# A Fourier mixing and gated feed-forward kernel: the third of the first-level products is split again

## Chip, cores and metric

The kernel runs on one core of one Trainium2 chip. The metric is device time in microseconds (us).

## What is computed

```python
X = np.fft.fft(x, axis=1)              # x: (8, 3008, 256) float32
X = np.fft.fft(X, axis=2)
x2 = X.real.reshape(24064, 256)
h = x2 @ w_in                          # w_in: (256, 2048)
g = h * (1.0 / (1.0 + np.exp(-1.702 * h)))
out = g @ w_out                        # w_out: (2048, 256)
```

## The kernel before

The second Fourier transform is folded into `w_in` once, at the start (`wcs`). The first one is done for batch b+1 while the feed-forward of batch b runs, in small matmul groups: first-transform groups (`mix1`, four per batch) and second-transform groups (`stage2`, three per batch, one for each block of output frequencies). `rotate` (the column turn) fixes one column of the first transform's result with a small matmul and a copy by ScalarE before the next batch's first `stage2`.

The main loop runs over 384 steps t = (batch b, block blk, half hh, p). Eight steps, p = 0 to 7, make a group: one output tile of 256 frequency columns (226 in the groups with blk 0 and hh 1, called narrow below) and their mirror columns. A step computes two blocks of 128 hidden features for both sides, and what it adds to the output is done LAG = 3 steps later. Steps 0 to 7 and the last eight work in simpler ways; steps 8 to 375 are called deep: 46 groups, 184 pairs of steps.

In a step t each engine has its own queue, in program order:

- TensorE (PE): `begin(t, 1)` and `begin(t + 1, 0)`, the two halves of the hidden matmuls into the PSUM banks x (tags b0 and b1, by turns); `product(t - 3)`; the small products of a pair; a transform group, if the step has one.
- ScalarE (ACT): `forward` (L649), `doubled` (L646), `activate_back` (L656), then `middle(t + 2)` (L634, twice), which writes the bank x of step t + 2 with a starting value. It can do so only when `backward(t)` has read that bank.
- VectorE (DVE): `backward(t)` (L653) subtracts to give the mirror side; `sums` (L671, L672) makes the sums S2 and S4 of a pair of steps; `deeper` makes the second-level sums, in two parts (L695 and L697, then L699 one step later).
- GpSimd: `sums` (L664, L665) makes S1 and S3; the folds of the first transform.

The output matmul uses products by the seven-for-eight scheme (Strassen's in Winograd's form), on 2 by 2 blocks. At the first level there are seven products per step: of A11, S2, S3 with weights each 128 by 128, and of the four operands A12, S4, A22, S1. For those four the pair of steps is split again in the same way: `small_products` does seven products (numbered 1 to 7) of 64 by 128 blocks for each of them, from the raw halves of operands and from the sums in `big[SUM:]`. They add up in the PSUM tile `low` (three banks) and part of bank o1 during a group. The first three are done by `product`, on all 256 columns.

At a group's end `combine` copies and adds the first-level results (L810, L813, L814); in the next step, the one whose product opens the next group, `combine_small` reads the second-level results from `low` (L842, four operations). `swap` (L850 to L852, ScalarE) exchanges partition halves; `combine_last` (L824, L860), `turn_last` and `store` finish two to four steps later.

Transform groups need PSUM banks for a short time. They take the banks of `low`, and bank b2, in the second step of a group, when `low` has just been read. Nearly every group has one there. Such a step is called special; in it the small products of the running pair are put off, and the step after it (`after`) does all seven at once. 36 of the 46 group ends are followed by a special step (21 hold a `stage2`, 13 two `mix1`, one a `mix1`, one a `stage2` and a `mix1`), 10 are not. The order is written out by hand; nothing reorders it.

## Time and profile before

| | |
|---|---|
| median of 3 runs | 1838.43 us (1836.69 to 1840.38) |
| the profiled execution | 1838.17 us, its span 1836.0 us |
| granted TensorE clock, mean | 1.0 |
| VectorE, busy | 1476.7 us, 80% |
| ScalarE, busy | 1137.6 us, 62% |
| GpSimd, busy | 991.0 us, 54% |
| L653 (`backward`), waiting for ScalarE's L649 | 143.0 us, 174 times |
| L695 (`deeper`), waiting for small products | 86.6 us, 115 times |
| L842 (`combine_small`), waiting for small products | 31.6 us, 45 times |

Busy times are those of one execution. A matmul is shown with the span from its start to its modelled end, and they overlap; what a group of them takes is read from the start of one group to the start of the next. A float32 matmul shows as two instructions in the counts. DVE and ScalarE operations also overlap their neighbour a little, so the same holds there. Idle time of an engine that isn't the bottleneck costs nothing.

### The profile page before, as it was taken

Reading aid. Unit: us, or ns where it says so; the run is one execution under the profiler, and the core shown is the slowest. Engines: PE = TensorE matmul, PEld = TensorE weight load, DVE = VectorE, ACT = ScalarE, POOL = GpSimd, SP = SyncE. Lnnn points to the kernel's source line nnn. Section 1 sums busy time; section 2 is a strip of 40 time slices with the busy share of each in tenths; the row PEclk is TensorE's granted clock in tenths of the full one; section 3 lists DMA queues with packets and bytes.
Section 4 is the critical chain, followed back from the end, with each engine's and each line's share of the span. In section 5 each row is a group of like instructions: output and inputs, shape, how many; then the busy total and the mean of one; then the engine's idle time right before and its main releaser. Section 6 shows DMA issues by size and latency. Waiting matters only on the chain.

```text
span 1836.0 us, 55861 instructions
## 1 busy us (share of the span) xinstructions
PE 1820.3 (99%) x23656; PEld 1403.6 (76%) x23656; DVE 1476.7 (80%) x1927; ACT 1137.6 (62%) x2238; POOL 991.0 (54%) x1070
## 2 busy tenths in 40 slices
PE   8999999999999999999999999999999999999998
PEld 5677778777777777777778777787777877777775
DVE  7988878887888778887887878878788787878874
ACT  4566656666666656666666666666665666656663
POOL 3785556553656546565456644666446653444442
PEclk9999999999999999999999999999999999999999
DMA  8811160214211151212402024020331102100011
GB/s 272 195 52 35 44 115 20 64 26 100 56 48 36 42 117 23 61 35 67 88 13 75 24 67 86 15 80 18 86 67 30 31 18 65 29 20 13 18 24 24
DMA packets 151687, 105.68 MB, mean 58 GB/s; under 512 B 106212, under 2 KB 133094, under 8 KB 150878
## 3 DMA queue, kind: packets, MB, share of 16 engines
q1 hardware_dynamic: 148270, 99.09, 22.3%
q8 instruction: 186, 3.05, 0.7%
q10 hardware_dynamic: 3168, 3.03, 0.6%
q14 instruction: 63, 0.52, 0.1%
HBM read 64.81 MB, written 48.05 MB: 61 GB/s over the span
## 4 chain that ended last, share of the span: by engine, by line
PE 96%; DMA 2%; DVE 1%; ACT 0%; issue 0%; POOL 0%; DVEq 0%; ACTq 0%; POOLq 0%
PE x L196 35%; PE o L196 27%; PE low L740 25%; PE o L740 4%; PE low L273 1%; PE low L393 1%; DMA big<-in_moe_w_in_dram 1%; DMA xt<-in_x_dram 1%; PE po L196 0%; PE pa L196 0%; PE pb L196 0%; POOL xt L905 0%; DVE big L751 0%; PE low L196 0%; PE psw L533 0%
## 5 line engine op out<-in xcount | busy, mean ns | idle before, releaser
L664 POOL TENSOR_TENSOR big<-big 128x256 f32<-128x256 f32 (+1 forms) x376 | 364.7, 970 | 787.6 <-ACT big L656 776.9
L196 PE MATMUL x<-pq,wcs 128*64 128x256 f32 (+1 forms) x6016 | 769.7, 375 | 0.4 <-ACT x L634 0.4
L196 PE MATMUL o<-big,wo 128*64 128x256 f32 (+1 forms) x4800 | 635.3, 376 | 0.3 <-DVE big L671 0.3
L196 PEld LDWEIGHTS x<-pq,wcs 128*64 128x64 f32 x6016 | 427.0, 137 | 172.6 <-issue 1.2
L196 PEld LDWEIGHTS o<-big,wo 128*64 128x64 f32 x4800 | 340.3, 137 | 146.6 <-issue 10.0
L646 ACT ACTIVATE g<-x 128x512 f32<-128x512 f32 (+1 forms) x376 | 221.7, 590 | 363.5 <-PE x L196 362.4
L665 POOL TENSOR_TENSOR big<-big 128x256 f32<-128x256 f32 (+1 forms) x376 | 381.1, 1014 | 0.0
L740 PE MATMUL low<-big 128*64 128x128 f32 (+1 forms) x5888 | 379.8, 270 | 0.0
L649 ACT ACTIVATE big<-x 128x512 f32<-128x512 f32 (+1 forms) x376 | 221.8, 590 | 237.4 <-PE x L196 211.3
L653 DVE TENSOR_TENSOR big<-g,x 128x512 f32<-128x512 f32 (+1 forms) x376 | 250.8, 667 | 143.4 <-ACT big L649 143.0
L634 ACT ACTIVATE x<-nb,af 128x256 f32<-128x256 f32 (+1 forms) x752 | 352.7, 469 | 12.2
L740 PEld LDWEIGHTS low<-big 128*64 128x64 f32 x5888 | 337.2, 137 | 24.7
L695 DVE TENSOR_TENSOR big<-big 128x1024 f32<-128x1024 f32 (+1 forms) x184 | 225.2, 1224 | 108.4 <-PE low L740 86.6
L656 ACT ACTIVATE big<-big 128x512 f32<-128x512 f32 (+1 forms) x376 | 231.5, 616 | 27.4 <-DVE big L653 26.1
L740 PE MATMUL low<-big,wo 128*64 128x128 f32 (+1 forms) x2944 | 222.4, 270 | 0.1
L699 DVE TENSOR_TENSOR big<-big 128x512 f32<-128x512 f32 (+1 forms) x184 | 191.6, 1041 | 0.0
L740 PEld LDWEIGHTS low<-big,wo 128*64 128x64 f32 x2944 | 174.4, 137 | 6.6 <-DVE big L699 0.6
L697 DVE TENSOR_TENSOR big<-big 128x512 f32<-128x512 f32 (+1 forms) x184 | 166.6, 906 | 16.0
L672 DVE TENSOR_TENSOR big<-big 128x512 f32<-128x512 f32 (+1 forms) x188 | 158.9, 845 | 6.5
L842 DVE TENSOR_TENSOR big<-big,low 128x512 f32<-128x512 f32 (+3 forms) x184 | 109.1, 610 | 35.1 <-PE low L740 31.6
L671 DVE TENSOR_TENSOR big<-big 128x512 f32<-128x512 f32 (+1 forms) x188 | 131.6, 700 | 0.9 <-POOL big L664 0.9
L740 PE MATMUL o<-big,wo 128*64 128x128 f32 (+1 forms) x1472 | 111.2, 270 | 0.0
(119 smaller groups left out, 1105.1 us busy)
## 6 DMA issues: line engine op xcount, KB each, us to landing
out_dram<-os SPq DMA_DIRECT2D x284, 64.0 KB
Td<-xt SPq DMA_DIRECT2D x56, 192.0 KB
t<-Td SPq DMA_DIRECT2D x21, 512.0 KB
xt<-in_x_dram SPq DMA_DIRECT2D x14, 512.0 KB
xt<-Xr SPq DMA_DIRECT2D x14, 512.0 KB
nb<-Nd SPq DMA_DIRECT2D x22, 256.0 KB
out_dram<-os SPq DMA_DIRECT2D x96, 56.0 KB
Xr<-in_x_dram SPq DMA_DIRECT2D x7, 752.0 KB
```

The source lines that it names most:

```text
L196: nc.tensor.matmul(out[c0:c0 + 64], lhsT=lhs[:, c0:c0 + 64], rhs=rhs, skip_group_check=True, **how)
L634: nc.scalar.activation(x[:, i * 256:i * 256 + n], nbt[b, blk][:, hh * 256:hh * 256 + n], ACTF.Copy, scale=af1[:, f:f + 1])
L646: nc.scalar.activation(two(g[:], n), two(xb[t][:], n), ACTF.Copy, scale=2.0)
L649: nc.scalar.activation(front(t), two(xb[t][:], width(t)), ACTF.Gelu_apprx_sigmoid)
L653: nc.vector.tensor_tensor(back(t), two(gt.pop(t)[:], n), two(xb.pop(t)[:], n), op=ALU.subtract)
L656: nc.scalar.activation(back(t), back(t), ACTF.Gelu_apprx_sigmoid)
L664: eng.tensor_tensor(right(t, S1, n), left(t, A21, n), right(t, A22, n), op=ALU.add)
L665: eng.tensor_tensor(left(t, S3, n), left(t, A11, n), left(t, A21, n), op=ALU.subtract)
L695: nc.vector.tensor_tensor(free(big[:], SUM, *both_), free(big[:], from11 + w, *twice), free(big[:], from11, [at_right(t, 0) + w - from11, ...
L697: nc.vector.tensor_tensor(s2, a11, s1, op=ALU.subtract)
L699: nc.vector.tensor_tensor(s4, a12, s2, op=ALU.subtract)
L740: nc.tensor.matmul(o, lhsT=lhs, rhs=rhs, start=first_in, stop=(p == NP - 2), skip_group_check=True)
```

## The change

The product of S3 also goes to the second level. S3 moves from the left operands to the right ones (five operands for four in `raws`, `made_sum` and `deeper`), with its own seven small products, `lone_products`. They fill one PSUM bank, `lone`, which is the bank b2; product 7 is split into two column halves, so that each side of the array gets the same work. `lone_weights` makes the weight sums once. At a group's end `move_lone` (seven ScalarE copies) and `combine_lone` (five VectorE operations) put the result together into the output sum, and `combine_last` gets one more addition. `combine` loses one (L814) in deep groups. Transform groups now take `low` and `lone`; `rotate` stands ahead of `stage2` in the special step itself. The output tile has one buffer for two, and the back operand two slots for four. The core of the diff:

```diff
-    op = ctx.enter_context(tc.tile_pool(name="op", bufs=2, space=SB))
+    op = ctx.enter_context(tc.tile_pool(name="op", bufs=1, space=SB))
...
-    LEFT, MADE, RIGHT, SUM, RES, OUT = 0, 4096, 8192, 14336, 16384, 18432
-    A11, A21, S3, S2 = range(4)
-    A12, S4, A22, S1 = range(4)
+    LEFT, BACK, OUT, SPARE, MADE, RIGHT, SUM, RES = 0, 2048, 2560, 3584, 4096, 8192, 15872, 18432
+    A11, S2 = range(2)
+    A12, S4, A22, S1, S3 = range(5)
...
+    def at_back(t):
+        return BACK + t % 2 * 256
...
-            eng.tensor_tensor(right(t, S1, n), left(t, A21, n), right(t, A22, n), op=ALU.add)
-            eng.tensor_tensor(left(t, S3, n), left(t, A11, n), left(t, A21, n), op=ALU.subtract)
+            a21 = big[:, at_back(t):at_back(t) + n]
+            eng.tensor_tensor(right(t, S1, n), a21, right(t, A22, n), op=ALU.add)
+            eng.tensor_tensor(right(t, S3, n), left(t, A11, n), a21, op=ALU.subtract)
...
-            both_, twice = ([512, 2], [128, 4], [1, w]), ([0, 2], [256, 4], [1, w])
+            both_, twice = ([640, 2], [128, 5], [1, w]), ([0, 2], [256, 5], [1, w])
             nc.vector.tensor_tensor(free(big[:], SUM, *both_), free(big[:], from11 + w, *twice),
-                                    free(big[:], from11, [at_right(t, 0) + w - from11, 2], [256, 4], [1, w]), op=ALU.subtract)
+                                    free(big[:], from11, [at_right(t, 0) + w - from11, 2], [256, 5], [1, w]), op=ALU.subtract)
...
+    ALONE = {2: (0, 0), 3: (0, 1), 4: (128, 0), 5: (128, 1), 1: (256, 0), 6: (256, 1), 7: (384, 0)}
+
+    def lone_products(t, ks):
...
+        for k in ks:
+            c0, side = ALONE[k]
...
+            part = (w + 1) // 2
+            for side_, lo, hi in ((0, 0, part), (1, part, w)) if k == 7 else ((side, 0, w),):
+                nc.tensor.matmul(pot["lone"][64 * side_:64 * side_ + 64, c0:c0 + hi - lo], lhsT=lhs, rhs=rhs[:, lo:hi],
+                                 start=opens(p, 5, side_), stop=(p == NP - 2), skip_group_check=True)
...
-            plan = [(0, 0, wo[:, p, 0, :], left(t, A11, n)), (0, 1, wt[:, p, 0, :], left(t, S2, n)),
-                    (1, 0, wt[:, p, 1, :], left(t, S3, n))]
+            plan = [(0, 0, wo[:, p, 0, :], left(t, A11, n)), (0, 1, wt[:, p, 0, :], left(t, S2, n))]
...
+    def move_lone(t):
...
+        nc.scalar.copy(across[64:128], ps[0:64, 256:256 + w])
+        nc.scalar.copy(across[0:64], ps[64:128, 256:256 + w])
+        nc.scalar.copy(begun[0:64], ps[0:64, 256:256 + w])
+        for to in (0, 64):
+            nc.scalar.copy(whole[to:to + 64, 0:part], ps[0:64, 384:384 + part])
+            nc.scalar.copy(whole[to:to + 64, part:], ps[64:128, 384:384 + w - part])
+
+    def combine_lone(t):
...
+        nc.vector.tensor_tensor(u, across, ps[:, 256:256 + w], op=ALU.add)
+        nc.vector.tensor_tensor(begun[64:128], u[64:128], ps[64:128, 128:128 + w], op=ALU.add)
+        nc.vector.tensor_tensor(u, u, whole, op=ALU.add)
+        nc.vector.tensor_tensor(oc[:, 2, 0:w], begun, ps[:, 0:w], op=ALU.add)
+        nc.vector.tensor_tensor(oc[:, 2, w:2 * w], u, ps[:, 128:128 + w], op=ALU.add)
...
@@ def combine_last(t):
+        nc.vector.tensor_tensor(oc[:, 2, :n], oc[:, 1, :n], oc[:, 2, :n], op=ALU.add)
         fifth(free(big[:], RES + 768, [0, 2], [1, n]), n)
...
@@ main loop
+            if t > NP:
+                spare[:] = ["l0", "l1", "l2", "l3"]
+                for fn, args in extra.get(t, ()):
+                    if fn is rotate:
+                        fn(*args)
...
             if opening:
                 small_products(t - LAG - 1, other[:2])
+                lone_products(t - LAG - 1, (1, 6))
...
             if not after:
                 small_products(t - LAG - 1, other[2 * opening:])
+                lone_products(t - LAG - 1, (2, 3) if opening else (1, 6, 2, 3))
...
             if after:
                 small_products(t - LAG - 1, (7, *other, 1, 2, 4))
+                lone_products(t - LAG - 1, (7, 1, 6, 2, 3, 4, 5))
             elif not special:
                 small_products(t - LAG, one)
+                lone_products(t - LAG, (7, 4, 5))
...
+            if t == seconds_late:
+                nyquist(1, 0, f"b{t % 2}")
             if t + 2 < n:
                 middle(t + 2)
+            move_lone(t - LAG - 1)
...
             combine_small(t - LAG - 1)
+            combine_lone(t - LAG - 1)
...
             sums(t - 1, nc.vector)
             turn_seconds()
             deeper(t - 2, 0)
             deeper(t - 3, 1)
```

## Prediction

> **What bounds the kernel now.** I read the page first, then the list of waits of each engine, then the timelines of DVE, ScalarE and TensorE around one group end. The page:
>
> ```profile
> span 1836.0 us, 55861 instructions
> ...
> PE 1820.3 (99%) x23656; PEld 1403.6 (76%) x23656; DVE 1476.7 (80%) x1927; ACT 1137.6 (62%) x2238; POOL 991.0 (54%) x1070
> ...
> PE 96%; DMA 2%; DVE 1%; ACT 0%; issue 0%; POOL 0%; DVEq 0%; ACTq 0%; POOLq 0%
> ```
>
> TensorE (PE) sets the end: busy 1820.3 of 1836.0 us, 96% of the chain. Less matmul work shortens the run only where PE still never waits, so the question is how near the other engines are to making it wait. DVE is next, at 80%; an average hides clumps. Its clump is at a group end. Call S the step whose product opens a new group, T3 the moment when PE reaches the first hidden matmuls of step S+3 (in step S+2). One such place, DVE, ScalarE and PE timelines (start, duration):
>
> ```profile
> 729.80 2.46 DVE L842 TENSOR_TENSOR big<-big,low 128x512 f32<-128x512 f32 x4 [0.80 <-PE low L740]
> 732.18 1.22 DVE L695 TENSOR_TENSOR big<-big 128x1024 f32<-128x1024 f32 x1
> 733.43 0.69 DVE L697 TENSOR_TENSOR big<-big 128x512 f32<-128x512 f32 x1
> 734.04 0.68 DVE L653 TENSOR_TENSOR big<-g,x 128x512 f32<-128x512 f32 x1
> ...
> 740.61 1.03 DVE L697 TENSOR_TENSOR big<-big 128x512 f32<-128x512 f32 x1
> 741.57 1.21 DVE L824 TENSOR_TENSOR big<-big 128x512 f32<-128x512 f32 x1
> ```
>
> ```profile
> 734.76 0.63 ACT L656 ACTIVATE big<-big 128x512 f32<-128x512 f32 x1 [0.41 <-DVE big L653]
> 735.30 0.97 ACT L634 ACTIVATE x<-nb,af 128x256 f32<-128x256 f32 x2
> ```
>
> ```profile
> 729.15 0.61 PE L740 MATMUL low<-big,wo 128*64 128x128 f32 x8
> 729.59 1.46 PE L196 MATMUL o<-big,wo 128*64 128x256 f32 x12
> 730.88 1.03 PE L196 MATMUL x<-pq,wcs 128*64 128x256 f32 x8
> 731.74 1.03 PE L196 MATMUL o<-big,wo 128*64 128x256 f32 x8
> 732.61 1.03 PE L196 MATMUL x<-pq,wcs 128*64 128x256 f32 x8
> ...
> 736.90 1.03 PE L196 MATMUL x<-pq,wcs 128*64 128x256 f32 x8
> ```
>
> DVE runs without a gap from 729.80 to the subtraction of step S+1 (L653, 734.04); that frees an x bank; ScalarE, in order, does L656 and then the two L634 that prefill the bank, ending at 736.27; PE wants it at 736.90. The chain is hidden by 0.63 us. It is the same place in every group. From the trace I took the end of the second L634 and the start of the matmuls: the cover (median) is 0.73 us where step S+1 holds a second-transform group, 1.40 where it holds two first-transform groups (1.05 in the 226-wide groups), 0.67 where it holds neither; in an ordinary step 1.2.
>
> **PE: what the change saves.** Per pair of deep steps the S3 product goes from 8 matmul instructions on 256 columns (0.865 us for eight, 731.74 to 732.61) to 12 on 128 columns (0.44 us for eight, 729.15 to 729.59) and 4 on 64. No row has 64 columns; bounds are the one-column matmuls of `first_row` (16 in 0.58 us, 26 ns each) and the 128-column ones, 55 ns. I take 28, since half of 55 is above that floor. After: 12 × 55 + 4 × 28 = 0.77; saved 0.093 us per pair (0.10 to none at the two ends). 152 pairs of 256 and 32 of 226 give 14.1 + 2.6 = 16.8 us.
>
> **DVE and ScalarE: what it adds at each pair.** The three sums of `deeper` handle five operands for four. From L697's 0.69 for 512 and L695's 1.22 for 1024, one element costs 1.04 ns: +0.27 for the first, +0.13 each for the others. In ordinary steps DVE waits 0.8 us for PE ahead of L695, or 0.3 to 2 us for ScalarE ahead of L653, which covers it. If that cover were gone, 184 × 0.53 = 98 us is the price. GpSimd does the same two operations per step; its L665 ends over 2 us before the L653 that will now wait for it, two steps on.
>
> **What it adds at a group end.** Between L842 and the sums stand five new DVE operations on 128 columns. L842 takes 0.414 for 256 and 0.687 for 512, so 0.28 each; each but one depends on the one before (start to start up to 0.1 more, as L824 to L860 shows beyond its length). I take 1.35 for the five, between 1.0 (0.2 each) and 1.6. The first waits for seven small ScalarE copies; these follow L634 (ending 1.62 us after L842 began) and take 0.26 (128 columns, from 0.365 for 256 and 0.585 for 512) and 0.2, overlapping by 0.1 as L810 and L812 do: about 0.85, so ready at 2.5; 0.17 us lost against 2.38. With 0.27 + 0.13 for the longer sums, step S+1's subtraction comes 1.93 us later after L842's start: 6.17 for 4.24. ScalarE's 2.22 us to the end of L634 follow, and 0.05 to PE.
>
> PE meanwhile gets there sooner: after the last small product that starts L842 it lacks two S3 halves of 0.43 us in S and S+1 and has two lone products (0.21) more: 0.65 earlier in steps with transform groups (their lone products are put off to S+2), 0.33 without (another 0.32 of lone products). So PE's wait at T3 is 1.93 + 0.65 + 0.05 − cover:
> - second-transform group alone, 21 group ends: 1.90 × 20, and 0.36 for the first (cover 2.27): 38.4
> - two first-transform groups, 13: 1.23 × 7, and 1.35 × 6 in narrow ones (1.75 + 0.60 + 0.05 − 1.05): 16.7
> - one first-transform group, or one of each, in the first batch: 2.09 + 1.46 = 3.6
> - neither, 10: there ScalarE, not DVE, ended 0.44 later, so the cover is 1.11: 1.20 × 8, 1.55 for a narrow one, nothing for the last, which has no sums behind it: 11.2
>
> Sum 69.9 us. The wait for the S2 sum (L671) in the same step ends before this one, and the column turn's wait for L842, some 0.6 us seven times, lies ahead of T3 within it: no cost of their own.
>
> **A second wait.** Where S+1 held transform groups, S+2 does all small products and then all seven lone ones, and the lone one that reads the second sum comes last. The next pair's first sum overwrites it, and so waits until T3 + 0.865 + 3.07 + 0.75 + 0.2 = 4.9 us; now it starts at T3 + 2.4 (739.28). Behind it on DVE stand the second sum, a new 256-wide add (0.45), L824, L860 and the subtraction of S+3: 1.56 + 0.75 + 0.45 + 0.79 + 0.88, start at T3 + 9.3, bank prefilled at 11.6. PE reaches the matmuls of S+5 at T3 + 6.40 + 4.65 = 11.05. Wait 0.54; with rows as slow as the 1.03 and 1.21 above, which run beside GpSimd, 1.4. I take 0.6, since most of these DVE operations move out of GpSimd's stretch: 35 × 0.6 = 21 us (0 to 49).
>
> The Trainium skill (SBUF — State Buffer, Who interferes with whom) says that a DVE operation with two SBUF inputs is blocked for the whole of a GpSimd instruction that reads SBUF. The rows agree (0.69 alone, 1.03 beside L665), and by that rule the second wait would stand nearer its upper end, 1943 for the total.
>
> **Small things.** The last output group's fourth bank is now the lone bank, free only after the new adds: 1.7 us once. Sixteen 64-column weight sums in steps 6 to 16: 0 to 4 us, DVE has pauses there; I take 1. The single output buffer, the moved Nyquist bank and the fewer banks for transforms: no cost; the stores of a group leave within a step or two of eight, and the third and fourth bank are wanted 0.5 us after the new adds end. The turn issues no DMA and passes none on SP or GpSimd.
>
> **Sum.** The profiled execution took 1838.17 us (span 1836.0), 0.26 under the median. 1838.2 − 16.8 + 69.9 + 21 + 1.7 + 1 = 1915 us.
>
> **Rivals.**
> 1. The cover holds and PE stays the bound: 1838.2 − 16.8 = 1821. For: DVE is at 80%, and PE waits nowhere now. Against: the cover of 0.63 to 1.4 us must take 1.93 of DVE and 0.65 of earlier PE. The point: the change is faster only if DVE's 1.93 us are under some 0.75. The longer sums alone are 0.40, so five adds would have to cost 0.35. Chance 0.06; an even result 0.02.
> 2. DVE does not catch up before the next group end and bounds everything: busy 1476.7 + 98 + 46 × 1.4 = 1639, and if its present idle time (359 us) is all forced by order, 1998. Against: counted on from T3 as above, the prefill for S+6 is ready 1 us ahead again. Chance 0.04.
> 3. PE falls back to half speed after each wait. At the start, after idling, its 512-column matmuls stand 0.853 us apart for 5.3 us, then 0.43: 2.65 lost. Times 45 that is 119 on top, 2034. Against: after a wait of 1.86 us at 55.2 matmuls ran at full pace at once. Chance 0.015. The Trainium skill (TensorE: Matmul & The Clock Gate, Part 1: The HAM clock gate) has it halve after an idle window of about 3.4 us; by that rule waits of 2 us leave it whole, and the row at 55.2 agrees.
> 4. The change doesn't do what it says: one-sided products of 64 weight columns don't overlap as pairs. Then a pair's 0.77 doubles: + 142, 2057. Against: the order alternates sides as `halves` does. Chance 0.015.
>
> **Numbers.** Forecast 0.85. Its ends: adds at 1.0 and no second wait, 1915 − 16 − 21 = 1878; adds at 1.6 and GpSimd's stretch met, 1915 + 11 + 21 = 1947. The range 1866 to 1946 goes a little past the low end for what may hide more. A measurement can tell 0.2% (3.7 us) from no change. Faster 0.06, same 0.02, slower 0.92.
>
> **What would show it.** Right: PE busy about 1803 of 1913 us (94%), with 45 to 80 waits of its x matmuls for ScalarE's prefill, 1 to 2 us each; the five adds near 1.35 us per group; the subtraction of S+1 6.2 us after L842's successor starts. Wrong: PE still at 99% (rival 1); waits at every step (rival 2); granted clock under 1.0 (rival 3); PE busy time up (rival 4). The forecast fails most simply if the five adds cost under half of what I took.

## The result and the profile after

| | before | after |
|---|---|---|
| median of 3 runs, us | 1838.43 (1836.69 to 1840.38) | 2032.53 (2032.11 to 2038.53) |
| ratio | | 1.1065, 95% interval 1.1029 to 1.1102 |
| profiled execution, us (span) | 1838.17 (1836.0) | 2038.53 (2036.7) |
| granted TensorE clock, mean | 1.0 | 0.987 |

The change made the kernel slower, by 10.65% as the ratio has it; the medians differ by 194 us, where 77 were forecast. The profile page after, with the lines that answer to those of before:

```profile
span 2036.7 us, 59380 instructions
...
PE 1888.5 (93%) x25128; PEld 1430.5 (70%) x25128; DVE 1703.4 (84%) x2173; ACT 1211.4 (59%) x2560; POOL 1085.9 (53%) x1070
...
PE 48%; DVE 26%; ACT 16%; issue 7%; DMA 2%; POOL 1%; DVEq 0%; SPq 0%; ACTq 0%; POOLq 0%
```

PE had 96% of the chain that ends last, and has 48% now; DVE and ScalarE (ACT) have most of the rest. No engine is full: PE is busy for 93% of the span, DVE for 84%. What was lost are waits. From the list of waits (who waited for whom: us in total, times, longest); the line by itself is from the list before, and answers to the first:

```profile
ACT big L663 <- DVE big L660: 287.3, 184, 3.8
...
PEld o L198 <- DVE big L679: 103.1, 100, 2.6
DVE big L703 <- PE lone L747: 101.5, 32, 4.4
...
DVE big L911 <- ACT big L903: 35.5, 46, 0.9
```

```profile
ACT big L656 <- DVE big L653: 26.1, 49, 2.2
```

(L842, L695, L697, L699, L653, L656, L634 and L671 of before are L885, L703, L705, L707, L660, L663, L641 and L679 now. L649 `forward` and L646 `doubled` are L656 and L653 now, GpSimd's L664 and L665 are L672 and L673, the move of a transform out of `low`, L403 of before, is L405.) One group end with a second-transform group alone behind it, DVE's timeline (start, duration, operation, and in brackets the idle time before it):

```profile
805.04 2.45 DVE L885 TENSOR_TENSOR big<-big,low 128x512 f32<-128x512 f32 x4
808.29 0.29 DVE L911 TENSOR_TENSOR big<-big,lone 128x128 f32<-128x128 f32 x1 [0.80 <-ACT big L903]
...
809.46 0.28 DVE L915 TENSOR_TENSOR big<-big,lone 128x128 f32<-128x128 f32 x1
809.66 1.48 DVE L703 TENSOR_TENSOR big<-big 128x1280 f32<-128x1280 f32 x1
811.18 0.82 DVE L705 TENSOR_TENSOR big<-big 128x640 f32<-128x640 f32 x1
811.92 0.68 DVE L660 TENSOR_TENSOR big<-g,x 128x512 f32<-128x512 f32 x1
812.52 0.68 DVE L679 TENSOR_TENSOR big<-big 128x512 f32<-128x512 f32 x1
...
819.33 1.49 DVE L703 TENSOR_TENSOR big<-big 128x1280 f32<-128x1280 f32 x1 [2.84 <-PE lone L747]
...
828.20 3.72 DVE L703 TENSOR_TENSOR big<-big 128x1280 f32<-128x1280 f32 x1
```

Three things are to be seen. The first add waits 0.80 us for the last of the seven copies, so the subtraction (L660) starts 6.88 us after L885; it was 4.24 before. The next sum of five (819.33) waits 2.84 us for the lone products. And the sum of five after that (828.20) takes 3.72 us instead of 1.48. On PE in the same group:

```profile
810.53 0.60 PE L198 MATMUL o<-big,wo 128*64 128x256 f32 x4
813.26 0.65 PE L198 MATMUL o<-big,wo 128*64 128x256 f32 x4 [2.12 <-DVE big L679]
814.20 1.08 PE L198 MATMUL x<-pq,wcs 128*64 128x256 f32 x8 [0.29 <-ACT x L641]
```

T3, the start of the `x` matmuls, stands at 814.20: 9.16 us after L885, where it was 7.10. Without the waits PE would have been there at 811.39 (810.53 and two times 0.43).

To see where the time went I took, from both traces, the start of the second hidden matmuls of each step (`begin(t, 1)`) and compared each step's length with the same step's before. Means per group end, in us longer than before (the two groups in the first batch with one first-transform group are in the last line alone):

| groups | S | S+1 | S+2 | S+3 | S+4 | S+5 | S+6 | S+7 |
|---|---|---|---|---|---|---|---|---|
| second-transform group alone (21) | 0.22 | -0.18 | 3.51 | -0.10 | 0.53 | -0.10 | 0.61 | -0.10 |
| two first-transform groups (13) | 0.27 | 0.68 | 2.06 | -0.09 | 1.75 | -0.09 | 0.41 | -0.08 |
| no transform (9) | 0.01 | 1.64 | 0.60 | -0.09 | 0.23 | -0.09 | 0.49 | -0.09 |
| all 45, us in total | 8.4 | 19.2 | 113.5 | -4.3 | 37.1 | -4.2 | 22.6 | -4.2 |

Steps S+3, S+5 and S+7 are shorter by 0.08 to 0.10 us, which is a pair's whole saving on PE; the steps between them are not, and S+2 alone lost 113.5 us. The table adds up to 188 us. The two profiled executions differ by 200.7: 5.7 us more lie in steps 8 to 19, 4.7 in the last group and 2.0 ahead of step 8.

### The profile page after: what moved, and what is told of

The parts are those of the page before. It is cut to its first block, busy times and chain, and to the rows that moved or that the text cites. A ratio compares the mean times of both kernels' runs of the same rounds, so it can differ in the third digit from the quotient of the medians.

```text
span 2036.7 us, 59380 instructions
## 1 busy us (share of the span) xinstructions
PE 1888.5 (93%) x25128; PEld 1430.5 (70%) x25128; DVE 1703.4 (84%) x2173; ACT 1211.4 (59%) x2560; POOL 1085.9 (53%) x1070
## 3 DMA queue, kind: packets, MB, share of 16 engines
q8 instruction: 198, 3.24, 0.7%
## 4 chain that ended last, share of the span: by engine, by line
PE 48%; DVE 26%; ACT 16%; issue 7%; DMA 2%; POOL 1%; DVEq 0%; SPq 0%; ACTq 0%; POOLq 0%
PE x L198 18%; PE low L776 16%; DVE big L703 8%; PE o L198 6%; ACT x L641 6%; DVE big L660 5%; PE lone L747 5%; ACT big L663 4%; PE o L776 3%; DVE big L705 2%; DVE big L707 2%; DVE os L836 1%; DVE big L867 1%; ACT g L653 1%; ACT xt L282 1%
## 5 line engine op out<-in xcount | busy, mean ns | idle before, releaser
L672 POOL TENSOR_TENSOR big<-big 128x256 f32<-128x256 f32 (+1 forms) x376 | 383.6, 1020 | 892.3 <-ACT big L663 892.2
L198 PE MATMUL x<-pq,wcs 128*64 128x256 f32 (+1 forms) x6016 | 781.1, 381 | 39.4 <-ACT x L641 29.3
L198 PEld LDWEIGHTS x<-pq,wcs 128*64 128x64 f32 x6016 | 408.8, 138 | 244.2 <-ACT x L641 81.7
L198 PE MATMUL o<-big,wo 128*64 128x256 f32 (+1 forms) x3328 | 439.4, 380 | 64.2 <-DVE big L679 63.0
L703 DVE TENSOR_TENSOR big<-big 128x1280 f32<-128x1280 f32 (+1 forms) x184 | 334.8, 1819 | 137.1 <-PE lone L747 101.5
L663 ACT ACTIVATE big<-big 128x512 f32<-128x512 f32 (+1 forms) x376 | 233.1, 620 | 291.4 <-DVE big L660 287.3
L653 ACT ACTIVATE g<-x 128x512 f32<-128x512 f32 (+1 forms) x376 | 221.7, 590 | 305.1 <-PE x L198 303.7
L673 POOL TENSOR_TENSOR big<-big 128x256 f32<-128x256 f32 (+1 forms) x376 | 392.8, 1045 | 0.0
L198 PEld LDWEIGHTS o<-big,wo 128*64 128x64 f32 x3328 | 231.5, 138 | 194.6 <-DVE big L679 103.1
L641 ACT ACTIVATE x<-nb,af 128x256 f32<-128x256 f32 (+1 forms) x752 | 350.9, 467 | 12.2
L656 ACT ACTIVATE big<-x 128x512 f32<-128x512 f32 (+1 forms) x376 | 220.0, 585 | 148.4 <-PE x L198 109.0
L660 DVE TENSOR_TENSOR big<-g,x 128x512 f32<-128x512 f32 (+1 forms) x376 | 248.6, 661 | 62.0 <-ACT big L656 59.5
L707 DVE TENSOR_TENSOR big<-big 128x640 f32<-128x640 f32 (+1 forms) x184 | 234.5, 1275 | 0.0
L705 DVE TENSOR_TENSOR big<-big 128x640 f32<-128x640 f32 (+1 forms) x184 | 201.6, 1096 | 13.4
L747 PE MATMUL lone<-big,wo 128*64 128x128 f32 (+3 forms) x2944 | 203.8, 258 | 0.0
L680 DVE TENSOR_TENSOR big<-big 128x512 f32<-128x512 f32 (+1 forms) x188 | 154.8, 824 | 6.5
L747 PEld LDWEIGHTS lone<-big,wo 128*64 128x64 f32 x2944 | 153.3, 137 | 0.0
L679 DVE TENSOR_TENSOR big<-big 128x512 f32<-128x512 f32 (+1 forms) x188 | 132.8, 707 | 6.1 <-POOL big L672 6.1
```

Of the source, the lines that this page charges most:

```text
L198: nc.tensor.matmul(out[c0:c0 + 64], lhsT=lhs[:, c0:c0 + 64], rhs=rhs, skip_group_check=True, **how)
L641: nc.scalar.activation(x[:, i * 256:i * 256 + n], nbt[b, blk][:, hh * 256:hh * 256 + n], ACTF.Copy, scale=af1[:, f:f + 1])
L653: nc.scalar.activation(two(g[:], n), two(xb[t][:], n), ACTF.Copy, scale=2.0)
L660: nc.vector.tensor_tensor(back(t), two(gt.pop(t)[:], n), two(xb.pop(t)[:], n), op=ALU.subtract)
L663: nc.scalar.activation(back(t), back(t), ACTF.Gelu_apprx_sigmoid)
L672: eng.tensor_tensor(right(t, S1, n), a21, right(t, A22, n), op=ALU.add)
```

## Experiments

All times are medians; ratios are to the kernel before, run on the same chip. "Theory" letters are those of the expectations.

| kernel | us | ratio (95% interval) |
|---|---|---|
| no_adds | 1926.46 | 1.0466 (1.0435 to 1.0496) |
| four_sums | 1950.01 | 1.0594 (1.0563 to 1.0624) |
| lone_early | 1993.92 | 1.0832 (1.0801 to 1.0864) |
| no_copies | 1984.25 | 1.0787 (1.0756 to 1.0819) |
| kept_busy | 2138.07 | 1.1615 (1.1582 to 1.1649) |
| kept_busy2 | 2028.58 | 1.1028 (1.0996 to 1.1061) |
| bare | 1847.92 | 1.0045 (1.0029 to 1.0061) |
| sums_only | 1872.64 | 1.0183 (1.0166 to 1.0200) |
| later_early | 1973.96 | 1.0731 (1.0686 to 1.0777) |
| first_early | 1965.75 | 1.0687 (1.0656 to 1.0718) |
| best | 1968.91 | 1.0706 (1.0688 to 1.0724) |
| kept_bank | 1934.74 | 1.0523 (1.0507 to 1.0540) |

**The group end: copies and adds.**

```diff
-            move_lone(t - LAG - 1)
...
-            combine_lone(t - LAG - 1)
```

(and L932 stays, but reads one part of the output sum twice, since the other is no longer made)

> Left out: the putting together of the fifth output sum at a group's end (the seven copies on ScalarE, L898 to L903, and the five adds on VectorE, L911 to L915); every product of the second level, its sums and its transfers stay. Theory A (what stands ahead of the next step's subtraction at a group's end sets the waits): the 45 group ends go back to about 4.6 us from the group's last copy to that subtraction instead of 6.9, the wait at the transform matmuls two steps on goes down from about 2.1 to under 0.7 us, and with it the half-clock windows there: 90 to 115 us off, 1915 to 1940 us. Theory B (VectorE has become too slow everywhere, because its sums of five collide with GpSimd): only the 1.4 us of adds per group are saved at most, and part of that is hidden: under 45 us off, 1985 to 2015 us. Theory C (the lone product that comes last in its step holds up the sums four steps after the group's end): that wait stays about 2.8 us whichever of the two holds.

1926.46 us, 106 less: theory A's range, and beyond what B allowed. In the same group the subtraction now starts 4.63 us after L885, and the first of PE's two waits is gone; the lines for DVE and PE:

```profile
767.61 2.44 DVE L885 TENSOR_TENSOR big<-big,low 128x512 f32<-128x512 f32 x4
769.98 1.48 DVE L703 TENSOR_TENSOR big<-big 128x1280 f32<-128x1280 f32 x1
771.50 0.82 DVE L705 TENSOR_TENSOR big<-big 128x640 f32<-128x640 f32 x1
772.24 0.68 DVE L660 TENSOR_TENSOR big<-g,x 128x512 f32<-128x512 f32 x1
```

```profile
773.12 1.11 PE L198 MATMUL o<-big,wo 128*64 128x256 f32 x8
774.51 1.08 PE L198 MATMUL x<-pq,wcs 128*64 128x256 f32 x8 [0.28 <-ACT x L641]
```

The steps S+4 and S+6 were as long as with the change (39.2 and 22.6 us in all), as theory C has it. Of the half-clock stretches described below, none is left in the steps for 14 in the change, so the clock's part is within the 106.

The copies alone were left out next, the adds kept:

```diff
-            move_lone(t - LAG - 1)
```

> Left out: the seven copies on ScalarE at a group's end (L898 to L903); the five adds on VectorE stay and read what stands in those places. What it tells apart is how the 106 us that went without copies and adds divide. Theory A1 (the copies run one after the other for 1.6 us and hold the first add back by 0.8 us, and the adds themselves take 1.4 us): the wait for L903 goes, the subtraction comes 6.1 us after the group's last sum step begins instead of 6.9, 0.8 x 45 = 36 us off, and with shorter waits most of the half-clock windows too (15 of them, 1.5 us each): 40 to 62 us off, 1970 to 1993 us. Rival (the copies' lateness only takes the place of a wait for something else, such as the transform matmuls' first operand on ScalarE): under 20 us off.

1984.25 us, 48 less, theory A1. The subtraction comes at 5.99 us after L885, T3 at 8.27. Beside the other kernels this makes a plain rule. Medians of the 21 groups with a second-transform group alone, us after the start of L885:

| | subtraction (L660) | T3 |
|---|---|---|
| before | 4.24 | 7.10 |
| bare (below) | 4.24 | 6.51 |
| no_adds | 4.63 | 6.90 |
| no_copies | 5.99 | 8.27 |
| the change | 6.88 | 9.15 |

In these groups T3 is the subtraction plus 2.27 us everywhere but before: that is ScalarE's L663 and the two L641 behind it. Before, PE came 0.59 us later than that.

**The order of the lone products.**

```diff
-                small_products(t - LAG - 1, (7, *other, 1, 2, 4))
-                lone_products(t - LAG - 1, (7, 1, 6, 2, 3, 4, 5))
+                small_products(t - LAG - 1, (7, 5))
+                lone_products(t - LAG - 1, (7, 4, 5))
+                small_products(t - LAG - 1, (6, 3))
+                lone_products(t - LAG - 1, (1, 6, 2, 3))
+                small_products(t - LAG - 1, (1, 2, 4))
```

> Nothing left out. In the step in which a pair's products come after the transform matmuls, the lone products that read the pair's made sums come among the first, and the small products of the raw operands last, so that the buffer of sums comes free earlier. Theory C (the lone product 5 that comes last holds up the next sums, and by them the step four after a group's end): VectorE's wait of 2.84 us in step S+2 goes below 1, the wait at the matmuls of step S+4 goes, 37 us are at stake there and 10 to 22 us two steps on: 20 to 45 us off, 1988 to 2012 us. Rival (the sums four steps after a group's end are late because of GpSimd and not because of the product): the wait moves to another instruction, and under 8 us come off.

1993.92 us, 39 less, with nothing left out: theory C. DVE's wait of 2.84 us is 0.20 now:

```profile
797.07 0.68 DVE L660 TENSOR_TENSOR big<-g,x 128x512 f32<-128x512 f32 x1
797.95 1.49 DVE L703 TENSOR_TENSOR big<-big 128x1280 f32<-128x1280 f32 x1 [0.20 <-PE lone L747]
```

In the 21 groups S+4 and S+6 went to 0.00, in the 13 with two first-transform groups S+4 went from 1.75 to 0.92; S+2 stayed (112.1 us in all). So the late product was behind both later waits: it made DVE late, and being late its next long sums met a stretch of GpSimd. That stretch, in the change, stands beside the 3.72 us at 828.20 (GpSimd is POOL here):

```profile
827.92 1.27 POOL L249 TENSOR_TENSOR xt<-xt 111x510 f32<-111x510 f32 x1
829.15 0.73 POOL L672 TENSOR_TENSOR big<-big 128x256 f32<-128x256 f32 x1
829.84 0.72 POOL L673 TENSOR_TENSOR big<-big 128x256 f32<-128x256 f32 x1
```

L703 began during L249; L249, L672 and L673 follow each other to 830.56, and L703 ended at 831.92, 1.36 later, which is a little less than its length alone. So it seems to have advanced hardly at all before the third had ended; GpSimd's spans are rough. In the change 18 of 152 such sums took over 3 us, with the early order 9, and none before.

**The sums of five.**

```diff
-            both_, twice = ([640, 2], [128, 5], [1, w]), ([0, 2], [256, 5], [1, w])
+            both_, twice = ([640, 2], [128, 4], [1, w]), ([0, 2], [256, 4], [1, w])
```

(and 4 for 5 likewise in `raws`, `made_sum` and the second operand)

> Left out: the deeper sums for the fifth output sum (L703, L705 and L707 make sums of four operands as in the kernel before, and the lone products read what stands in those columns). Group ends, copies and products stay as they are. Theory A (the group's end sets the waits): the steps after a group's end lose only the difference of the sum that stands ahead of the subtraction, 1.49 to about 1.20 us, so 0.3 us x 45 = 13 us there, and the stalls that a longer first sum runs into beside GpSimd four and six steps on shrink by half: 25 to 45 us off, about 1990 to 2008 us. Theory B (VectorE too slow everywhere): 184 x 0.53 = 98 us of work go, and 70 to 98 us of it come off the time: 1935 to 1963 us.

1950.01 us, 82 less: in theory B's range, not in A's. This was a miss: I had counted only the 0.3 us at the group's end and half of the stretches beside GpSimd. S+4 went from 37.1 to 10.8 us, S+6 from 22.6 to 2.9, S+2 from 113.5 to 86.3. But B's reason is not thereby shown, for steps S+3, S+5 and S+7 are 0.09 us shorter in this kernel and in the change alike: DVE is not late everywhere. The two kernels that follow tell what these sums cost by themselves.

**All that is added beside PE, left out.** Beside the edits of no_adds, four_sums and lone_early:

```diff
-        nc.vector.tensor_tensor(oc[:, 2, :n], oc[:, 1, :n], oc[:, 2, :n], op=ALU.add)
...
-        at(t, lone_weights, i)
```

> Left out: all that the change adds beside TensorE's products: copies, adds and L932 at a group's end, the fifth operand of the deeper sums, the sums of weights (lone_weights), and the lone products stand early. The matmuls are all there, so what remains is the saving on TensorE (the step of the prediction that takes 16.8 us off) and the changed banks and places. Theory A (every bit of the 194 us comes from the added work on VectorE and ScalarE and from the order of the lone products): 1820 to 1830 us, faster than the kernel before by 0.5 to 1.0%. Rival (the changed banks, the moved column turn or the matmuls of 64 columns cost something too): 1835 to 1860 us.

1847.92 us: slower than before by 0.45% (0.29 to 0.61), so it is the rival's number and not A's. The 45 groups, from step 19 to the last, took 1698.5 us in bare and 1690.6 before, where 16 us less were forecast. The page shows PE busy for 98% again, and no long waits are left, yet the saving did not come out:

```profile
span 1847.6 us, 58724 instructions
...
PE 1817.5 (98%) x25128; PEld 1441.8 (78%) x25128; DVE 1463.1 (79%) x1881; ACT 1135.8 (61%) x2238; POOL 977.1 (53%) x1070
```

The chain to T3 is hardly the reason: there PE comes 0.59 us sooner, where 0.65 were forecast (6.51 for 7.10), which is 0.06 a group. The trace shows three other places. The column turn, which stands in the special step now, waits for L885 in seven groups; the change has this wait too, within its longer one:

```profile
PE low L198 <- DVE big L885: 4.3, 7, 0.6
```

Behind T3 the small products wait for the move of the transform out of `low` (L405): in the 21 groups with a second-transform group alone they start 0.05 us after its end (median), 0.14 us later after T3 than before. And in the six narrow groups with two first-transform groups S+4 is 1.2 us longer, 7 us in all. In each of them DVE's first sum of step S+2 waits for ScalarE; before, that wait stood two steps later, and PE did not wait for it. After it DVE runs without a gap up to the sum that PE waits for in S+4 (L679). The sum in one such group, in bare and then before:

```profile
783.85 1.10 DVE L703 TENSOR_TENSOR big<-big 128x904 f32<-128x904 f32 x1 [2.42 <-ACT big L663]
```

```profile
785.71 1.10 DVE L695 TENSOR_TENSOR big<-big 128x904 f32<-128x904 f32 x1 [1.53 <-ACT big L656]
```

The change also moves the three slots of a pair's operands on by two; whether that moved this wait was not tried. In the groups without a transform nearly the whole saving is there (-0.09 in S+3, S+5 and S+7, 0 to 0.10 in the others).

The same kernel with the sums of five put back:

```diff
-            both_, twice = ([640, 2], [128, 4], [1, w]), ([0, 2], [256, 4], [1, w])
+            both_, twice = ([640, 2], [128, 5], [1, w]), ([0, 2], [256, 5], [1, w])
```

> Left out as in bare: copies, adds and L932 at a group's end, and lone_weights; the lone products stand early; but the deeper sums have five operands again. It prices the sums of five alone, on top of bare's 1848. Theory A (the parts shorten the same few steps and overlap only a little: no copies and adds 106 us less, lone products early 38, each measured by itself): 1848 plus some 35 to 50 us, 1883 to 1898 us, nearly all of it in the steps two, four and six after a group's end. Rival (VectorE is late everywhere once its sums are longer): 1848 plus 80 to 98 us, 1928 to 1946 us, as four_sums took 82 us off the whole change.

1872.64 us, 25 more than bare: below theory A's range, and far from the rival's 80 to 98. So the same sums cost 25 us when the other additions are gone, and 82 when they are there.

**The granted clock.** In the profile after, 14 stretches of 3.41 us within the steps have half the clock, 13 of them just behind a group end. One of them, and the same place at a group end that escaped (the stretch, its length, PE busy, granted clock, DMA share, GB/s):

```profile
566.26:569.67 3.41, 3.41 (x30) 0.50 0.00 1
813.20:816.61 3.41, 3.06 (x38) 1.00 0.03 8
```

PE's timeline around the first:

```profile
564.86 0.65 PE L198 MATMUL o<-big,wo 128*64 128x256 f32 x4 [2.12 <-DVE big L679]
565.80 1.57 PE L198 MATMUL x<-pq,wcs 128*64 128x256 f32 x8 [0.28 <-ACT x L641]
567.14 2.72 PE L776 MATMUL low<-big 128*64 128x128 f32 x24
```

The wait of 2.12 us is the same in both, and so is what runs after it; at half clock the 24 small products take 2.72 us, at full clock 1.53 (815.21 in the other group). Two kernels put work into the wait:

```diff
+            elif after and all(fn is not mix1 for fn, _ in extra.get(t - 1, ())):
+                product(t - LAG, 0, 1)
+                for _ in range(2):
+                    nc.tensor.matmul(pot["low"][:, 1024:1536], lhsT=wcs[0][:, 0:128], rhs=wcs[0][:, 0:512], start=True, stop=True, skip_group_check=True)
+                product(t - LAG, 1, cut)
```

> Nothing left out, two matmuls of 512 columns with no use are added ahead of the waiting product in the step two after a group's end, in those groups whose next step holds one stage-2 transform alone (21 of 46); they fill about 0.5 us of each wait there with work. Theory D (TensorE's granted clock falls to half for one window of 3.41 us when the wait of about 2 us falls across the window's grid; 14 or 15 such windows in the profile, about 1.5 us each): the half-clock windows at these places go, and 12 to 20 us come off: 2012 to 2020 us. Rival (the windows follow the length of the wait alone or cost nothing): the windows stay, within 5 us of 2032, or longer by up to 10 us where the added matmuls themselves are late.

2138.07 us, 106 more, so this kernel tells nothing of theory D: the added matmuls waited themselves, since the transform group still stood in the bank that I gave them (PE and its weight loads at that line waited 79.1 and 89.1 us for L405).

```diff
-                    nc.tensor.matmul(pot["low"][:, 1024:1536], lhsT=wcs[0][:, 0:128], rhs=wcs[0][:, 0:512], start=True, stop=True, skip_group_check=True)
+                    nc.tensor.matmul(pot["lone"][:, 0:512], lhsT=wcs[0][:, 0:128], rhs=wcs[0][:, 0:512], start=True, stop=True, skip_group_check=True)
```

> Nothing left out; as kept_busy, but the two added matmuls write the bank of the fifth sum, which nobody reads or writes at that time, instead of a bank out of which VectorE still had to move a transform: in kept_busy the added matmuls waited for that move (L405, 168 us in all), which is why it came to 2138. Here they fill 0.9 to 1.7 us of the 2.1 us of the wait in the 21 groups with one stage-2 transform. Theory D (the granted clock halves for a window of 3.41 us where the wait falls across the window's grid): the half-clock windows at these places go and 12 to 22 us come off: 2010 to 2020 us. Rival (the windows cost nothing, or come from the whole of the load and not from these waits): within 5 us of 2032.

2028.58 us, 4 less, which is the rival's number; the spans of the profiled executions are 2025.1 for 2036.7 us. The trace shows the added matmuls in the wait:

```profile
806.85 1.98 PE L1172 MATMUL lone<-wcs 128*128 128x512 f32 x4
809.03 0.65 PE L198 MATMUL o<-big,wo 128*64 128x256 f32 x4 [0.20 <-DVE big L679]
```

None of the 21 groups was hit any more, where 9 had been. Step S+2 of these nine had been 4.35 to 4.93 us longer than in the kernel before and was 3.24 to 3.39 longer now; group by group the difference is 1.0 to 1.5 us, 12.5 in all. That is theory D's mechanism, shown in the trace. Its 12 to 22 us are just missed by the spans (11.6) and missed by the medians (4). The profiled execution of the change had the lowest clock of its three (0.987, the others 0.989); against the other run of kept_busy2 (0.993) that is, as an estimate, five windows fewer, one window being 1.7 of some 2030 us; the two profiled executions have 14 and 6 in the steps.

**Other places for the same work.** Four kernels that leave nothing out move it.

```diff
             forward(t)
+            if not mixed_now:
+                move_lone(t - LAG - 2)
...
             sums(t - 1, nc.vector)
+            if not mixed_now:
+                combine_lone(t - LAG - 2)
```

(`mixed_now`: this step holds a first-level transform group; the same for `mixed_next` and the next step)

> Nothing left out. The lone products early as in lone_early, and the copies and adds of a group's end one step later, behind that step's subtraction and sums (not in the 14 groups whose next step holds two first-level transforms, which write the bank, and not in the last). Theory A (their place ahead of the subtraction is what costs): in the 30 groups with the later place the step two on lengthens as in the kernel without copies and adds, about 0.9 us instead of 3.5, 0.1 instead of 1.6 in groups without a transform: 60 to 85 us off lone_early's 1994, 1909 to 1934 us. Rival (VectorE has no room for 1.4 us anywhere in these two steps, so that the lateness only moves to the next subtraction): under 25 us off, 1970 to 1994 us.

1973.96 us, 20 less than lone_early: the rival. The adds now stood ahead of the move of the transform out of `low` (L405), and the small products behind that waited; in groups without a transform the copies stood ahead of L653. The waits:

```profile
PE low L776 <- DVE pq L405: 31.5, 22, 1.9
PE x L198 <- ACT g L653: 21.2, 16, 3.6
```

```diff
+            if t > NP and special:
+                deeper(t - 3, 0)
...
-            deeper(t - 2, 0)
+            if not special_next:
+                deeper(t - 2, 0)
```

> Nothing left out. As later_early, and in groups with a transform the sums of five (L703, L705) too stand behind the next step's subtraction and sums instead of ahead of them. Theory A: the 2.3 us of these sums leave the way to the subtraction, and the 0.9 us that the step two on still lengthens goes, and part of what the kernel before itself waited there: 20 to 45 us off later_early, 1870 to 1910 us. Rival (VectorE's work in the two steps, 11 us where TensorE needs about 9, is what counts, in whatever order): within 10 us of later_early, the wait one step later.

1965.75 us, 8 less again: the rival. In groups with two first-transform groups S+2 went from 2.1 to 0.9 us; in the 21 others it rose from 2.4 to 3.3 us: PE's wait for L405 grew from 31.5 to 45.8 us, and eight of them met a half-clock window, for one in later_early.

```diff
             backward(t)
+            if (t - LAG) % NP == 2:
+                if not mixed_past:
+                    combine_lone(t - LAG - 3)
+                lone_products(t - LAG - 1, (7, 4, 5, 1, 6, 2, 3))
```

> Nothing left out. In the 30 groups without a first-level transform next to their end the copies go behind the next step's scaled inputs on ScalarE (L641), the adds behind the subtraction two steps on, and the lone products of that step come last on TensorE; in the 14 with one, copies and adds stay and the sums of five go behind the next step's subtraction, as in first_early. later_early showed what its places ran into: in groups without a transform the copies held up L653 (1.26 us of wait at the matmuls), in those with a stage-2 transform the adds held up its move (L405) and the small products behind it (73 us in all). Theory A (the deadline that each operation is put ahead of sets the cost): st2 groups lengthen by 0.5 to 1.2 us, plain ones by 0.5 to 1.5, mixed ones by 1.9: 1880 to 1915 us. Rival (VectorE's work in two steps is what counts, wherever it stands): 1955 to 1975 us, as later_early and first_early.

1968.91 us: the rival, and not even better than first_early. S+2 fell to 1.1 us in the 21 groups as expected, but S+4 rose from 0 to 1.0 there: lone products that come last hold the S3 operands, and GpSimd wants to write the next ones:

```profile
POOL big L672 <- PE lone L747: 76.0, 19, 4.4
```

In groups without a transform S+2 is 2.6 us longer than in the kernel before: there the lone products themselves wait for the adds (PE for L915, 16.5 us in eight groups).

```diff
+        nc.scalar.copy(free(kept_lone[:], 0, [128, 2], [1, w]), free(ps[:], 128, [128, 2], [1, w]))
...
+            move_lone(t - LAG - 3)
...
+            combine_lone(t - LAG - 4)
...
-            combine_last(t - LAG - 3)
+            combine_last(t - LAG - 4)
```

> Nothing left out. At a group's end ScalarE moves the whole bank of the fifth sum into a buffer of its own (three copies), so that the bank is free at once; the copies between halves follow two steps later, the adds three steps later behind that step's subtraction, and what comes after them one step later too. Lone products early; the sums of five behind the subtraction in the groups with a first-level transform, as in first_early. Theory A (the adds cost because of what stands behind them at the group's end, and a calm step can take them): about what leaving them out gives together with the early lone products, 1885 to 1915 us. Rival (no step has room for them): 1950 to 1975 us, as later_early, first_early and best.

1934.74 us: 98 less than the change and 59 less than lone_early, the fastest kernel here that leaves nothing out, and slower than the kernel before by 5.2%. The number lies between the two ranges. Step S+2 is nearly as in no_adds (24.3 us in all, where it was 33.0), but S+5, two steps after the one that now holds the adds and the final sums, is 52.8 us longer in all. The waits of PE:

```profile
PE x L198 <- ACT x L641: 53.3, 56, 1.5
PE low L776 <- DVE big L707: 18.4, 20, 1.4
```

It is the same chain one step further on: the adds delay a subtraction, and the prefill (L641) comes late. So order and place matter, for half of the loss, and the rest was not got rid of by any place tried.

Put in a row, the 194 us read: 9 us for what is left in bare, 25 for the sums of five, 54 for the late lone order, `lone_weights` and L932 (from 1872.6 to no_adds), and 106 for copies and adds. The kernel before, run beside each, stood between 1838.4 and 1840.7, so each share is good to some 2 us. Another order of taking away gives other shares: alone, the adds are worth 106, the sums 82 and the order 39, which is 227 and more than the 185 that bare takes off with all of them.

## Why the prediction was wrong

The direction and the place of the first wait were right; the forecast of 1915 (1866 to 1946) was 117 us short. Step by step:

- **PE's saving, 0.093 us per pair.** Right: steps S+3, S+5 and S+7 are 0.08 to 0.10 us shorter in the change. Right too is how much sooner PE is at T3: in bare 0.59 us with a second-transform group, 0.65 with two first-transform groups and 0.31 with none, for 0.65, 0.65 and 0.33. That bare is still not faster is due to the places named there, the column turn and the narrow groups above all.
- **The group end, 69.9 us.** The mechanism was right: adds, sum of five, subtraction, ScalarE's prefill, T3. The mis-sized term is the seven copies, "about 0.85, ready at 2.5; 0.17 us lost". Only one pair of them overlaps by the 0.1 us that was taken for every pair (807.23 and 807.39):

```profile
806.68 0.26 ACT L898 COPY big<-lone 64x128 f32<-64x128 f32 x1
806.95 0.27 ACT L899 COPY big<-lone 64x128 f32<-64x128 f32 x1
807.23 0.26 ACT L900 COPY big<-lone 64x128 f32<-64x128 f32 x1
807.39 0.20 ACT L902 COPY big<-lone 64x64 f32<-64x64 f32 x1
807.61 0.21 ACT L903 COPY big<-lone 64x64 f32<-64x64 f32 x1
807.83 0.21 ACT L902 COPY big<-lone 64x64 f32<-64x64 f32 x1
808.05 0.21 ACT L903 COPY big<-lone 64x64 f32<-64x64 f32 x1
```

 All seven take 1.6 us and end 3.2 us after L885 began. The durations were right and the overlap was not. Subtraction at 6.88 for 6.17, T3 at 9.15 for 8.44: 0.71 × 46 = 33 us. The adds themselves took what was taken for them, 1.37 from 808.29 to 809.66 (1.35). In all, S+1 and S+2 lost 137 us (19.2 + 113.5, and the 4.2 that they should have saved), 67 more than forecast: 33 by the copies, 12 by the clock in nine groups, and 22 that are not shared out. Two waits in S+1 that the prediction does not have are among these:

```profile
PE low L776 <- DVE big L703: 11.3, 9, 1.5
PE x L198 <- ACT g L653: 9.8, 8, 2.2
```

 In groups without a transform the small products of the new pair wait for its first sum, which now stands behind the adds (9.8 us in eight of them). In the six narrow groups with two first-transform groups PE waits for L653 (6.9 us), which on ScalarE stands behind an L656 that waits for L703 (17.0 us).
- **The second wait, 21 us.** Its times were right in the groups it was worked out from: the sum of five starts 5.13 us after T3 (4.9 forecast), the subtraction of S+3 at 9.60 (9.3), and S+4 lost 0.53 (0.54 worked out, 0.6 taken). But it was taken for all 35 groups: with two first-transform groups it is 1.75. And it was taken as the last: S+6 and the next S lost another 23 and 8 us, where "counted on from T3" DVE had been held to be ahead again. In all 37 + 23 + 8 = 68 us for 21.
- **The cover of the longer sums in ordinary steps.** The step that failed there: "which covers it". The cover was the wait for PE; sums_only prices the longer sums at 25 us with the other additions gone, and four_sums at 82 with them there. A sum that runs into a stretch of GpSimd has no cover either. It was left to the upper bound of the second wait and should have been a term by itself. (That bound is 49 us for the 21 taken, so the upper end is 1954 and not 1947.) By the Trainium skill (SBUF — State Buffer, Who interferes with whom) an operation of DVE with two SBUF inputs contends with a GpSimd instruction that reads SBUF, and the shared ports are an exclusive lock. The row at 828.20 agrees, and goes further: it seems to have been shut out through three that followed each other.
- **The clock, rival 3.** Held at 0.015 and worked out at 119 us; it came true in 14 places, 9 of them 12 us together. That its total, 2034, lies beside the measured 2032.5 is chance: most of the loss is not the clock's. The row at 55.2 that spoke against it was one wait at one place of the windows' grid. The Trainium skill (TensorE: Matmul & The Clock Gate, Part 1: The HAM clock gate) says that the window is free-running and that the half clock comes after an idle window of about 3.4 us. The trace agrees with the grid; I read "idle window" as 3.4 us of idleness, and the trace shows that about 2.0 in one window are enough (below).
- **Small things.** `lone_weights` was taken at 1 us (0 to 4). Steps 8 to 19 took 54.9 us for 49.1, and 50.9 in sums_only, which lacks these weights: 4 us, the upper end; the longer sums are the other 2.
- **Rivals 1, 2, 4.** PE waits, so 1 fell. DVE catches up in every group (S+3, S+5 and S+7 are shorter), so 2 fell. The products of 64 weight columns pair as hoped, since the saving of 0.08 to 0.10 us is there, so 4 fell.

The sum of the misses, between the profiled executions: 67 at the group's end, 47 in the later waits, 5 in steps 8 to 19, and 5 in the last group and ahead of step 8 (6.7 for 1.7), which is the 124 us that 200.7 is above the forecast of 76.8. By the medians it is 117. The place of all of it is known; the cause of the 22 us above is not.

## What to carry to other kernels

An engine that runs at 99% without a wait hides chains that are just as long: before work is put on another engine, look for the chain that ends closest to it, add up what the change puts in front of it (here 2.6 us against a cover of 0.59 to 1.4), and take off the cover what the busy engine will come sooner, for a saving there uses it up (0.59 us in bare). Then follow the late engine to the end of its group: here a third of the loss came in steps after the first wait. Do not count small copies as overlapping because two others did: here that term was 0.7 us per group too small. Ask of every added read which buffer it holds and who writes that next: a product placed last in its step cost 39 us and putting it early cost nothing. And do not add up single experiments: 227 us of parts were 185 together.

## What the runs showed of the chip

- Half clock without an idle window. With the windows laid on the grid of the half-clock records (3.413 us), 12 of the 14 half-clock windows in the change follow one in which PE was idle for 1.96 to 2.50 us by the trace; among the windows that none follows, the most idle one has 1.80. In lone_early it is 2.01 to 2.40 against 1.99, in first_early 2.08 to 3.14 against 2.03. Two windows of the change follow only 1.1 and 1.2 us; both hold the 47-row matmuls of first-transform groups, and whether those count as less work was not tried. So the same wait of 2.1 us cost nothing more or 1.0 to 1.5 us more, by where it fell.
- Small copies on ScalarE from the `lone` bank: 64 columns take 0.21 us and start 0.22 apart, 128 columns take 0.26 and start 0.27 apart. Of the six pairs of neighbours one overlaps, by 0.10 us, in each of the 38 groups of 256 columns; what sets it apart was not tried.
- A DVE sum of two SBUF operands took 3.72 us for its 1.48 beside three GpSimd instructions that followed each other.
